# Strassen on column halves in the second layer of the last batch, with two subtractions done by adding transfers

## The chip, the cores and the metric

One NeuronCore of one Trainium2 chip runs the whole program. The metric is the device time of one execution in microseconds; three runs of the kernel before took 2145.92, 2146.27 and 2146.49 us, so the median is 2146.27 us. Engines are named as the profile names them: PE is TensorE (PEld its weight loads), DVE VectorE, ACT ScalarE, POOL GpSimd, and SP the engine that issues the ordinary DMA transfers.

## The reference

Attention over channels and then two dense layers. There are 4 batches of 6080 tokens with 256 channels:

```python
qn = q / (np.linalg.norm(q, axis=1, keepdims=True) + 1e-06)
kn = k / (np.linalg.norm(k, axis=1, keepdims=True) + 1e-06)
s = kn.transpose(0, 2, 1) @ qn / tau
a = np.exp(s - s.max(-1, keepdims=True))
a /= a.sum(-1, keepdims=True) + 1e-09
x = (v @ a).reshape(B * S, D)          # 24320 x 256
h = x @ w_in                           # 256 -> 2048
g = h - np.tanh(h)
return g @ w_out                       # 2048 -> 256
```

## The kernel before

The softmax matrix of a batch is folded into `w_in`, so that the first layer is one product of `v` with folded weights. All data are fp32; each operand of a large product is split into a high part `h` and a low part `l` (an ACT cast and a DVE subtraction), and one product is three matmuls: high weights by low data, high by high, low by high.

Tokens are taken in *pairs* of two column chunks: five *even* pairs of 512 + 512 tokens and one *uneven* pair of 512 + 448 per batch. The hidden layer is taken in 8 slices of 256. One slice of one pair is a *quad*: 2 x 2 blocks (row of 128 hidden units, column chunk of tokens), numbered 11, 12, 21 and 22. There are 4 x 6 x 8 = 192 quads. In the names, `x_3_2_4` is the buffer `x` of batch 3, pair 2, slice 4.

In a quad the first layer is done by Strassen's scheme: seven products p1 to p7 of three matmuls each (21 matmuls of 512 columns, in `products`, L314), accumulated in three PSUM banks X, Y and Z. `Quad.keep` (L1090, ACT) copies X into SBUF before the next product is added to it; `Quad.add` (L1100, DVE) adds such a copy to Y or Z and gives a chunk `c`; chunk 21 is left in X itself. `Quad.finish` turns a chunk into `g = c - tanh(c)`: tanh on ACT (L1112), subtraction on DVE (L1116), high part on ACT (L1120), low part on DVE (L1124). X and Z change between banks 0 and 2 from quad to quad, Y is bank 1.

The second layer (`second`, L1185) multiplies each of the four chunks of `g` by the rows of `w_out` that belong to it: 2 output halves x 3 matmuls of 512 columns, 24 in a quad. The sums over all 8 slices of a pair stay in banks 3 to 6, and are copied out (L1204) and stored (L1207) at its end. Bank 7 is for other work.

`Moving` brings in the tokens of a pair: a load of 1 MB (`vraw`), three subtractions that make `vt` (L882, L885, DVE), and seven splits into `v0` to `v6`.

The order of all instructions is laid down by a planner in the program itself: `ORDER` and `drain` mix the products of the first layer with matmuls of the second, which lags behind by `LAG` matmuls, and `Plan.order` walks through all operations with assumed costs and lists each engine's operations by assumed start. Each engine then runs its own list strictly in order, with semaphores between engines. Where an operation has to wait, all behind it on that engine wait too. In the last batch no attention work for a following batch is left.

Of the kernel before, what the change touches and what calls it, by code (L numbers as in the profile page):

```python
# [43 lines left out]
]  # L44
ENTER = 10
# [47 lines left out]
class Plan:  # L93
# [11 lines left out]
    LONG_LAG, BUSY = 4.5, 180.0  # L105

# [43 lines left out]
    def order(self):  # L150
        ops = self.ops
        for op in reversed(ops):
            if op.due is None:
                op.due = 1e9
            for d in op.deps:
                if d.engine != "PE" or d.fill:
                    d.due = min(1e9 if d.due is None else d.due, op.due - d.cost - self.LAG[d.engine] - self.HOP)
# [28 lines left out]
        while len(done) < len(ops):  # L186
# [66 lines left out]
def attn_moe(ctx: ExitStack, tc: tile.TileContext, qk, v4, qkT, tau, w_in, w_out, outT):  # L253
# [21 lines left out]
    pairs_of = [[*pairs[:MID], pairs[-1], *pairs[MID:-1]] if b + 1 < B else pairs for b in range(B)]  # L275
# [167 lines left out]
    factor = {}  # L443

# [30 lines left out]
    class Attn:  # L475
# [385 lines left out]
    class Moving:  # L861
# [15 lines left out]
        def sums(self, i):  # L877
            n = self.n
            r = self.raw[:, :, 0:n]
            if i == 0:  # L880
                self.t = sb(v_p, "vt", [P, 4, NMAX], F32, f"vt_{self.b}_{self.p}")
                nc.vector.tensor_sub(self.t[:, 0:2, 0:n], r[:, 1:3, :], r[:, 0:2, :])  # L882
            else:
                t = self.t[:, :, 0:n]
                nc.vector.tensor_sub(t[:, i + 1, :], r[:, i + 1, :], t[:, 0 if i == 1 else 2, :])  # L885
# [13 lines left out]
        def split_lo(self, i):  # L899
            nc.vector.tensor_sub(self.lo[i], self.source(i), self.hi[i].bitcast(F32))  # L900
# [133 lines left out]
    def plan_moving(i, after=()):  # L1034
# [3 lines left out]
        plan.add("SP", 0.35, v.load, writes=[raw], after=after, size=1.05)  # L1038
        for j in range(3):
            plan.add("DVE", dve_cost(n if j else 2 * n), lambda j=j: v.sums(j), reads=[raw], writes=[t])  # L1040
        vbuf[i] = {}
        for j in range(7):
            h = Buf(ring["vhl"])
# [3 lines left out]
            plan.add("DVE", dve_cost(v.width(j)), lambda j=j: v.split_lo(j), reads=[src, h], writes=[l])  # L1047
            vbuf[i][j] = h, l


    def banks(gs):

        return {"X": 2 * (gs % 2), "Y": 1, "Z": 2 - 2 * (gs % 2)}

    class Quad:
# [47 lines left out]

        def finish(self, i, c):

            n, name = self.ns[i % 10 - 1], f"{i}_{self.name}"
            t, h, l = Buf(ring["t"]), Buf(ring["gh"]), Buf(ring["gl"])
            self.bufs["g", i] = h, l

            def tanh():  # L1110
                self.tiles["t", i] = sb(g_p, "t", [P, NMAX], F32, f"t{name}")[:, 0:n]
                nc.scalar.activation(self.tiles["t", i], self.tiles[c][:, 0:n], AF.Tanh)  # L1112
# [44 lines left out]

    stream = []
    outs = {}
    obufs = {}  # L1160

    def second(quad, i):

        b, p, s = quad.b, quad.p, quad.s
# [16 lines left out]
        for m, part, x, j in parts:  # L1181
# [47 lines left out]
    for i in range(1, B * NP):  # L1229
        task(NS2 * i - 5, "start", lambda i=i: plan_moving(i, [plan.last_pe]))  # L1230
# [245 lines left out]
    current = None  # L1476
# [110 lines left out]
```

## Time and profile before

| | |
|---|---|
| median of 3 runs | 2146.27 us |
| profiled execution: span, first to last instruction | 2144.3 us |
| PE busy | 2139.4 us, 9666 matmuls |
| DVE busy | 1820.5 us |
| ACT busy | 1578.8 us |
| POOL busy | 37.1 us |
| granted TensorE clock (of 2.4 GHz) | 1.000 |

The page gives the profiled execution by its span alone; the median of the runs is 2.0 us above it. Busy times of DVE and ACT are sums of intervals in which an instruction is in the engine from start to end; the next one can start a little before that end. A busy PE is modelled, so whether PE waited is read from the distance of matmul starts, not from its share. Idle time of the engines beside PE costs nothing as long as PE goes on.

### The profile page before, as it was taken

Reading aid. Unit: us, or ns where it says so; the run is one execution under the profiler, and the core shown is the slowest. Engines: PE = TensorE matmul, PEld = TensorE weight load, DVE = VectorE, ACT = ScalarE, POOL = GpSimd, SP = SyncE. Lnnn points to the kernel's source line nnn. Section 1 sums busy time; section 2 is a strip of 40 time slices with the busy share of each in tenths; the row PEclk is TensorE's granted clock in tenths of the full one; section 3 lists DMA queues with packets and bytes.
Section 4 is the critical chain, followed back from the end, with each engine's and each line's share of the span. In section 5 each row is a group of like instructions: output and inputs, shape, how many; then the busy total and the mean of one; then the engine's idle time right before and its main releaser. Section 6 shows DMA issues by size and latency. Waiting matters only on the chain.

```text
span 2144.3 us, 28289 instructions
## 1 busy us (share of the span) xinstructions
PE 2139.4 (100%) x9666; PEld 1793.2 (84%) x9666; DVE 1820.5 (85%) x3094; ACT 1578.8 (74%) x2922; POOL 37.1 (2%) x37
## 2 busy tenths in 40 slices
PE   9999999999999999999999999999999999999999
PEld 8888888888888888888888888888888888888888
DVE  8998988888898888888889888888888978778776
ACT  6677878767777788886777788887677676666665
POOL 5100000000000000000000000000000000000000
PEclk9999999999999999999999999999999999999999
DMA  9845676355335576643633567564354332332331
GB/s 384 303 163 194 201 265 214 139 160 192 119 134 196 209 246 214 216 156 109 203 131 126 180 237 250 184 227 157 111 196 147 133 126 93 137 125 87 132 117 53
DMA packets 125458, 373.51 MB, mean 174 GB/s; under 512 B 18626, under 2 KB 60866, under 8 KB 122242
## 3 DMA queue, kind: packets, MB, share of 16 engines
q1 hardware_dynamic: 125314, 371.70, 49.3%
q8 instruction: 76, 1.25, 0.2%
q14 instruction: 68, 0.56, 0.1%
HBM read 308.22 MB, written 62.66 MB: 173 GB/s over the span
## 4 chain that ended last, share of the span: by engine, by line
PE 99%; DMA 0%; SPq 0%; ACT 0%; issue 0%
PE ps_o L1185 48%; PE x L314 25%; PE y L314 12%; PE z L314 7%; PE ps_s L314 3%; PE ps_s L602 2%; PE ps_s L600 1%; PE ps_w L314 1%; DMA vhl<-qk_dram 0%; SPq L542 0%; SPq L349 0%; PE ps_n L534 0%; ACT ob L1204 0%; PE ps_b L680 0%; PE ps_t L724 0%
## 5 line engine op out<-in xcount | busy, mean ns | idle before, releaser
L314 PE MATMUL x<-v,f 128*128 128x512 f32 (+1 forms) x2304 | 620.4, 389 | 0.0
L1185 PE MATMUL ps_o<-gh,wo_l 128*128 128x512 f32 (+1 forms) x1536 | 594.9, 387 | 0.0
L1185 PE MATMUL ps_o<-gh,wo_h 128*128 128x512 f32 (+1 forms) x1536 | 594.9, 387 | 0.0
L1124 DVE TENSOR_TENSOR gl<-t,gh 128x512 fp32r<-128x512 f32 (+1 forms) x768 | 508.0, 680 | 22.5 <-ACT gh L1120 20.6
L314 PEld LDWEIGHTS x<-v,f 128*128 128x128 f32 x2304 | 432.6, 188 | 86.3
L1120 ACT CAST gh<-t 128x512 fp32r<-128x512 f32 (+1 forms) x768 | 457.9, 617 | 33.7 <-DVE t L1116 22.7
L1185 PE MATMUL ps_o<-gl,wo_h 128*128 128x512 f32 (+1 forms) x1536 | 470.5, 387 | 0.0
L1112 ACT ACTIVATE t<-c 128x512 f32<-128x512 f32 (+1 forms) x576 | 359.3, 626 | 122.1 <-DVE c L1100 115.4
L1116 DVE TENSOR_TENSOR t<-c,t 128x512 f32<-128x512 f32 (+1 forms) x576 | 389.8, 680 | 37.3 <-ACT t L1112 28.3
L1090 ACT COPY u<-x 128x512 f32<-128x512 f32 (+1 forms) x384 | 221.9, 578 | 209.4 <-PE x L314 207.7
L1100 DVE TENSOR_TENSOR c<-u,y 128x512 f32<-128x512 f32 (+1 forms) x384 | 259.1, 675 | 113.1 <-ACT u L1090 75.2
L1185 PEld LDWEIGHTS ps_o<-gl,wo_h 128*128 128x128 f32 x1536 | 288.4, 188 | 57.2
L1185 PEld LDWEIGHTS ps_o<-gh,wo_l 128*128 128x128 f32 x1536 | 288.4, 188 | 56.3
L1185 PEld LDWEIGHTS ps_o<-gh,wo_h 128*128 128x128 f32 x1536 | 288.5, 188 | 56.2
L314 PE MATMUL y<-v,f 128*128 128x512 f32 (+1 forms) x1152 | 319.0, 385 | 0.0
L314 PEld LDWEIGHTS y<-v,f 128*128 128x128 f32 x1152 | 215.1, 188 | 40.3
L1112 ACT ACTIVATE t<-x 128x512 f32<-128x512 f32 x192 | 114.8, 598 | 133.4 <-PE x L314 132.6
L1116 DVE TENSOR_TENSOR t<-x,t 128x512 f32<-128x512 f32 x192 | 132.6, 691 | 73.1 <-ACT t L1112 72.4
L1100 DVE TENSOR_TENSOR c<-p,z 128x512 f32<-128x512 f32 x192 | 131.7, 686 | 49.1 <-PE z L314 45.6
L314 PE MATMUL z<-v,f 128*128 128x512 f32 x576 | 161.8, 389 | 0.0
L314 PEld LDWEIGHTS z<-v,f 128*128 128x128 f32 x576 | 108.1, 188 | 22.5
L1090 ACT COPY p<-x 128x512 f32<-128x512 f32 x192 | 112.7, 587 | 5.9 <-PE x L314 2.0
(168 smaller groups left out, 1455.2 us busy)
## 6 DMA issues: line engine op xcount, KB each, us to landing
f<-f_d SPq DMA_DIRECT2D x160, 896.0 KB, 4.6
raw<-qk_dram SPq DMA_DIRECT2D x104, 384.0 KB, 5.0
nt<-qkT_dram SPq DMA_DIRECT2D x96, 380.0 KB, 5.1
f_d<-f SPq DMA_DIRECT2D x32, 896.0 KB, 3.9
vraw<-v_dram SPq DMA_DIRECT2D x24, 1024.0 KB, 7.3
outT_dram<-ob SPq DMA_DIRECT2D x88, 256.0 KB, 3.2
wt<-wt_d SPq DMA_DIRECT2D x24, 512.0 KB, 6.8
wt<-wi_d SPq DMA_DIRECT2D x36, 256.0 KB, 5.1
```

The source lines that it names most:

```text
L314: ins = nc.tensor.matmul(out, w, x, start=first and i == 0, stop=last and i == len(seq) - 1, skip_group_check=True,)
L600: nc.tensor.matmul(self.ps[:, 0:C], x[:, 1, k], x[:, 0, q], start=False, stop=last, skip_group_check=True)
L602: nc.tensor.matmul(self.ps.rearrange("p (a c) -> p a c", a=2), x[:, 0, k], x[:, :, q], start=first, stop=False, skip_group_check=True,)
L1090: nc.scalar.copy(self.tiles[to], self.tiles["X"][:, 0:n])
L1100: nc.vector.tensor_add(self.tiles[i], self.tiles[u], self.tiles[ps][:, 0:n])
L1112: nc.scalar.activation(self.tiles["t", i], self.tiles[c][:, 0:n], AF.Tanh)
L1116: nc.vector.tensor_sub(x, self.tiles[c][:, 0:n], x)
L1120: nc.scalar.copy(self.g[i][0], self.tiles["t", i])
L1124: nc.vector.tensor_sub(self.g[i][1], self.tiles["t", i], self.g[i][0].bitcast(F32))
L1185: nc.tensor.matmul(outs[key + (m,)][:, 0:n], (wo_l if part else wo_h)[:, f, m * P:(m + 1) * P], quad.g[i][x], start=first and j == 0, stop ...
```

## The change

It concerns the 40 quads of the even pairs of the last batch (`halved`: batch 3, pair index above 0). For that the uneven pair of this batch is moved from its last place to its first.

The two chunks of the first column, 11 and 21, are taken together as a 2 x 2 block problem: two rows (slices of 128 hidden units) by two halves of 256 columns, against the 2 x 2 blocks of `w_out`. It is done by seven products of three matmuls with 256 columns (21 matmuls of 256 columns) in place of 12 matmuls of 512. The sums of weight blocks are made once in batch 0 (`Sums`), kept in DRAM, and loaded for each of the 40 quads (512 KB, `load_sums`). The sums of data blocks are four DVE subtractions of 256 columns a quad (`Quad.sums`, buffer `ts`). What is split into high and low parts is then `b1` (256 columns), `b2`, `t1` and `t2` (512 each) in place of `gh11/gl11` and `gh21/gl21`. The seven products are summed over the 8 slices in halves of banks 3, 4, 2 and 7, and at the end of a pair put together by two ACT copies and eight DVE additions of 256 columns (`gather_halves`). Banks 2 and 7 being taken, X is always bank 0, and Y and Z share bank 1.

For chunks 11 and 12 of these quads the subtraction `c - tanh(c)` is not done on DVE: ACT writes `-tanh(c)`, and a transfer issued by POOL adds `c` to it in SBUF (`join`, 256 KB).

```diff
+HALVES = [
+    ("p6", []), ("p2", [5, "c"]), ("p5", []), ("p7", [5]), ("p4", ["d", 3]), ("p3", ["a", 4]), ("p1", ["b", 5.5]),
+]
+JOINED = [(),(11,12)]
+SUMS_AT = 3 * 8
...
+    JOIN_LAG, JOIN_SHARE = 4.5, 1.45
...
-    pairs_of = [[*pairs[:MID], pairs[-1], *pairs[MID:-1]] if b + 1 < B else pairs for b in range(B)]
+    pairs_of = [[*pairs[:MID], pairs[-1], *pairs[MID:-1]] if b + 1 < B else [pairs[-1], *pairs[:-1]] for b in range(B)]
...
+        def whole(self):
...
+            nc.vector.tensor_add(self.w, wo_h[:, part].bitcast(F32), wo_l[:, part].bitcast(F32))
+        def sums(self):
...
+            nc.vector.tensor_add(y[:, 0], a21, a22)
+            nc.vector.tensor_sub(y[:, 1], y[:, 0], a11)
+            nc.vector.tensor_sub(y[:, 2], a11, a21)
+            nc.vector.tensor_sub(y[:, 3], a12, y[:, 1])
...
+    def load_sums(gs):
...
+        nc.sync.dma_start(so[gs].bitcast(F32), so_d[s].rearrange("p h (i m) -> p h i m", i=4))
...
-        def sums(self, i):
+        def sums(self, i, eng):
...
-                nc.vector.tensor_sub(self.t[:, 0:2, 0:n], r[:, 1:3, :], r[:, 0:2, :])
+                eng.tensor_sub(self.t[:, 0:2, 0:n], r[:, 1:3, :], r[:, 0:2, :])
...
+        name, cost, eng = ("DVE", dve_cost, nc.vector)
         for j in range(3):
-            plan.add("DVE", dve_cost(n if j else 2 * n), lambda j=j: v.sums(j), reads=[raw], writes=[t])
+            plan.add(name, cost(n if j else 2 * n), lambda j=j: v.sums(j, eng), reads=[raw], writes=[t])
...
+            if j not in POOLED:
+                name, cost, eng = "DVE", dve_cost, nc.vector
+            plan.add(name, cost(v.width(j)), lambda j=j, eng=eng: v.split_lo(j, eng), reads=[src, h], writes=[l])
+            if halved(i // NP, i % NP):
+                name, cost, eng = "POOL", pool_cost, nc.gpsimd
...
+    def halved(b, p):
+        return b == B - 1 and p > 0
...
+        if halved(*where(gs)[:2]):
+            return {"X": 0, "Y": 1, "Z": 1}
...
+                def join():
+                    nc.gpsimd.dma_start(self.tiles["n", i], self.tiles[c][:, 0:n], accum_op=ALU.add)
+                plan.add("ACT", act_cost(n), tanh, reads=[self.bufs[c]], writes=[g])
+                plan.add("POOL", 1.0, join, reads=[self.bufs[c]], writes=[g], port=False, lag=plan.JOIN_LAG)
...
+                    (y[:, 0], g(1, 1), g(1, 0)), (y[:, 1], g(2, 1), g(1, 1)), (y[:, 2], g(2, 1), y[:, 0]), (y[:, 3], g(2, 0), y[:, 2]),
+                )[i]
+                nc.vector.tensor_sub(out, a, b)
...
+    HALF_BANKS = {"p1": (3, 0), "p2": (3, 1), "p3": (4, 0), "p5": (4, 1), "p7": (2, 0), "p6": (2, 1), "p4": (7, 0)}
+    PRODUCTS = {
+        "b1": [("p1", (0, 0), 0)], "b2": [("p2", (1, 0), 0), ("p3", 3, 1)],
+        "t1": [("p5", 0, 0), ("p7", 2, 1)], "t2": [("p6", 1, 0), ("p4", (1, 1), 1)],
+    }
...
+                    nc.tensor.matmul(
+                        outs[b, p, place][:, at_ * HALF:(at_ + 1) * HALF], weights(a, part), quad.g[name][x][:, half * HALF:(half + 1) * HALF],
...
+        if halves_from - 4 <= gs < halves_from:
+            lag += 3
+        if gs == halves_from:
+            lag += 2
```

`lambda j=j: v.sums(j, eng)` reads `eng` when it runs, after the loop below it has set it to `nc.gpsimd` for the halved pairs: the three `vt` subtractions of a halved pair are planned as DVE work and issued on POOL.

How it moves instructions. On PE, from p6 to p7 of one quad (`x` by `v1` is p6, `z` p2, `y` by `v3` p5, `x` by `v4` p7; `ps_o` and `ps_h` are the second layer). Before:

```order
L314 MATMUL x_3_2_4_18959<-v1_3_2_18499,f_164_18814 128x512 x3
L314 MATMUL z_3_2_4_19000<-v2_3_2_18522,f_164_18814 128x512 x3
L1185 MATMUL ps_o_3_2_1_0_18764<-gh12_3_2_2_18915,wo_l_96 128x512
L1185 MATMUL ps_o_3_2_1_0_18764<-gh12_3_2_2_18915,wo_h_95 128x512
L1185 MATMUL ps_o_3_2_1_1_18769<-gh12_3_2_2_18915,wo_l_96 128x512
L1185 MATMUL ps_o_3_2_1_1_18769<-gh12_3_2_2_18915,wo_h_95 128x512
L314 MATMUL y_3_2_4_19016<-v3_3_2_18536,f_164_18814 128x512 x3
L1185 MATMUL ps_o_3_2_1_1_18769<-gl12_3_2_2_18926,wo_h_95 128x512
L1185 MATMUL ps_o_3_2_1_0_18764<-gl12_3_2_2_18926,wo_h_95 128x512
L314 MATMUL x_3_2_4_18959<-v4_3_2_18548,f_164_18814 128x512 x3
```

and now:

```order
L326 MATMUL x_3_2_4_19310<-v1_3_2_18337,f_164_19099 128x512 x3
L326 MATMUL z_3_2_4_19347<-v2_3_2_18195,f_164_19099 128x512 x3
L1376 MATMUL ps_h_3_2_4_19084<-t1_3_2_2_19239,sl_162_19138 128x256 x2
L1376 MATMUL ps_h_3_2_2_19115<-t1_3_2_2_19239,sl_162_19138 128x256 x3
L1376 MATMUL ps_h_3_2_2_19115<-t2_3_2_2_19276,sl_162_19138 128x256 x3
L1376 MATMUL ps_h_3_2_7_19127<-t2_3_2_2_19276,wo_h_95 128x256 x2
L326 MATMUL y_3_2_4_19370<-v3_3_2_18353,f_164_19099 128x512 x3
L326 MATMUL x_3_2_4_19310<-v4_3_2_18360,f_164_19099 128x512 x3
L1376 MATMUL ps_h_3_2_7_19127<-t2_3_2_2_19276,wo_l_96 128x256
```

Between p2 and p5 stand ten matmuls of 256 columns in place of four of 512, and p5 writes the bank that p2 wrote.

On DVE, from c12 of one quad to c11 of the next. Before:

```order
L1100 TENSOR_TENSOR c12_3_2_4_19073<-u2_3_2_4_19006,y_3_2_4_19016 128x512
L1124 TENSOR_TENSOR gl22_3_2_4_19080<-t22_3_2_4_19049,gh22_3_2_4_19069 128x512
L1124 TENSOR_TENSOR gl21_3_2_4_19086<-t21_3_2_4_19060,gh21_3_2_4_19075 128x512
L1116 TENSOR_TENSOR t12_3_2_4_19083<-c12_3_2_4_19073,t12_3_2_4_19083 128x512
L1100 TENSOR_TENSOR c11_3_2_5_19105<-p1_3_2_5_19066,z_3_2_5_19095 128x512
```

and now (`b2`, `glb1` and `gl22` are low parts, `ts` the sums of data halves, `n11` the chunk that the transfer of POOL has added to):

```order
L1166 TENSOR_TENSOR c12_3_3_3_20255<-u2_3_3_3_20186,y_3_3_3_20206 128x512
L1290 TENSOR_TENSOR t22_3_3_3_20249<-c22_3_3_3_20230,t22_3_3_3_20249 128x512
L1219 TENSOR_TENSOR b2_3_3_3_20258<-n21_3_3_3_20251,b2_3_3_3_20258 128x512
L1239 TENSOR_TENSOR ts_3_3_3_20276<-n11_3_3_3_20204 128x256
L1239 TENSOR_TENSOR ts_3_3_3_20276<-n21_3_3_3_20251,n11_3_3_3_20204 128x256
L1219 TENSOR_TENSOR glb1_3_3_3_20291<-n11_3_3_3_20204,ghb1_3_3_3_20280 128x256
L1239 TENSOR_TENSOR ts_3_3_3_20276<-n21_3_3_3_20251,ts_3_3_3_20276 128x256
L1298 TENSOR_TENSOR gl22_3_3_3_20302<-t22_3_3_3_20249,gh22_3_3_3_20285 128x512
L1166 TENSOR_TENSOR c11_3_3_4_20309<-p1_3_3_4_20271,z_3_3_4_20298 128x512
```

Between c12 and the next c11 stand seven operations in place of three, four of them of 256 columns.

`vt` and the transfers. Before, on DVE, where the tokens of pair 3 are prepared:

```order
L882 TENSOR_TENSOR vt_3_3_19004<-vraw_3_3_18906 128x1024
L1100 TENSOR_TENSOR c11_3_2_4_19014<-p1_3_2_4_18969,z_3_2_4_19000 128x512
L1124 TENSOR_TENSOR gl12_3_2_3_19020<-t12_3_2_3_18986,gh12_3_2_3_19009 128x512
L900 TENSOR_TENSOR v0_3_3_18992<-vraw_3_3_18906,v0_3_3_18992 128x512
L1116 TENSOR_TENSOR t11_3_2_4_19022<-c11_3_2_4_19014,t11_3_2_4_19022 128x512
L885 TENSOR_TENSOR vt_3_3_19004<-vraw_3_3_18906,vt_3_3_19004 128x512
```

and now, on POOL, where those of pair 4 are:

```order
L1181 DMA n11_3_3_2_20085<-c11_3_3_2_20068 128x512
L933 TENSOR_TENSOR vt_3_4_20103<-vraw_3_4_19923 128x1024
L1286 DMA t12_3_3_1_20099<-c12_3_3_1_20009 128x512
L936 TENSOR_TENSOR vt_3_4_20103<-vraw_3_4_19923,vt_3_4_20103 128x512
L1286 DMA t12_3_3_2_20149<-c12_3_3_2_20139 128x512
L1181 DMA n11_3_3_3_20204<-c11_3_3_3_20193 128x512
L1286 DMA t12_3_3_3_20266<-c12_3_3_3_20255 128x512
L936 TENSOR_TENSOR vt_3_4_20103<-vraw_3_4_19923,vt_3_4_20103 128x512
L1181 DMA n11_3_3_4_20319<-c11_3_3_4_20309 128x512
```

The three subtractions have gone to POOL, between two transfers a quad that this engine issues in order.

## Rows read from the trace of the kernel before

**Rows 1.** The page: span, busy time, PE clock, chain by engine.

```profile
span 2144.3 us, 28289 instructions
...
PE 2139.4 (100%) x9666; PEld 1793.2 (84%) x9666; DVE 1820.5 (85%) x3094; ACT 1578.8 (74%) x2922; POOL 37.1 (2%) x37
...
PEclk9999999999999999999999999999999999999999
...
PE 99%; DMA 0%; SPq 0%; ACT 0%; issue 0%
```

**Rows 2.** Chain of the last batch in time: start us, us, what, matmuls.

```profile
1991.48 1.36 PE x L314 x6
...
1999.64 2.04 PE ps_o L1185 x9
2001.68 1.36 PE x L314 x6
```

**Rows 3.** Windows: us, busy us of PE, PEld, DVE, ACT, POOL; PE clock, DMA share, GB/s.

```profile
140.00:180.00 40.00, 40.00 (x180) 33.19 (x179) 39.83 (x69) 31.70 (x60) 0.41 (x1) 1.00 0.44 155
...
430.00:600.00 170.00, 170.00 (x752) 140.81 (x751) 145.61 (x259) 119.47 (x211) 0.41 (x1) 1.00 0.46 154
770.00:870.00 100.00, 100.00 (x481) 86.74 (x481) 86.16 (x151) 82.47 (x170) 0.41 (x1) 1.00 0.65 221
...
1710.00:2060.00 350.00, 350.00 (x1545) 289.89 (x1544) 277.59 (x433) 238.01 (x419) 0.00 (x0) 1.00 0.33 119
```

**Rows 4.** Chain at the first folds, columns as in rows 2.

```profile
71.38 4.31 PE ps_w L314 x36
```

**Rows 5.** Groups by shape: line, engine, operation, names, shapes, count, busy us, mean ns.

```profile
L1124 DVE TENSOR_TENSOR gl<-t,gh 128x512 fp32r<-128x512 f32 x704 | 470.8, 686 | 15.2 <-ACT gh L1120 14.1
...
L882 DVE TENSOR_TENSOR vt<-vraw 128x1024 f32<-128x1024 f32 x24 | 29.3, 1220 | 0.0
...
L616 DVE TENSOR_TENSOR s<-s,ps_s 128x256 f32<-128x256 f32 x8 | 3.3, 416 | 0.0
...
L831 DVE TENSOR_TENSOR fx<-fx 128x128 f32<-128x128 f32 x32 | 9.1, 285 | 0.0
```

**Rows 6.** Timeline of one quad of the last batch: start us, us, engine, line, operation.

```profile
1999.68 0.59 ACT L1090 COPY u<-x 128x512 f32<-128x512 f32 x1 [1.30 <-PE x L314]
...
2000.30 0.69 DVE L1100 TENSOR_TENSOR c<-u,y 128x512 f32<-128x512 f32 x1 [1.20 <-ACT u L1090]
...
2001.02 0.63 ACT L1112 ACTIVATE t<-c 128x512 f32<-128x512 f32 x1 [0.23 <-DVE c L1100]
...
2001.52 1.52 PE L314 MATMUL x<-v,f 128*128 128x512 f32 x6
...
2002.46 0.60 ACT L1112 ACTIVATE t<-x 128x512 f32<-128x512 f32 x1 [0.81 <-PE x L314]
...
2003.09 0.69 DVE L1116 TENSOR_TENSOR t<-x,t 128x512 f32<-128x512 f32 x1 [0.71 <-ACT t L1112]
```

**Rows 7.** Timeline of POOL, columns as in rows 6.

```profile
41.22 1.38 POOL L373 TENSOR_TENSOR a_wi<-a_wi,m_wi 128x512 f32<-128x512 f32 x1 [2.73 <-DVE m_wi L370]
...
45.48 1.27 POOL L524 TENSOR_TENSOR acc<-vhl,acc 128x512 f32<-128x512 f32 x1
```

**Rows 8.** Timeline of DVE, columns as in rows 6.

```profile
41.52 1.64 DVE L363 SCALAR_TENSOR_TENSOR a_wi<-raw_wi,a_wi 128x512 int32<-128x512 int32 x1
43.08 3.67 DVE L524 TENSOR_TENSOR acc<-vhl,acc 128x512 f32<-128x512 f32 x6
```

**Rows 9.** DMA issues of 1700 to 2130 us: count, KB each, median us to landing.

```profile
f<-f_d SPq DMA_DIRECT2D x40, 896.0 KB, 4.5
outT_dram<-ob SPq DMA_DIRECT2D x20, 256.0 KB, 2.4
vraw<-v_dram SPq DMA_DIRECT2D x4, 1024.0 KB, 6.8
```

**Rows 10.** The page, DMA issues: columns as in rows 9.

```profile
wt<-wi_d SPq DMA_DIRECT2D x36, 256.0 KB, 5.1
```

**Rows 11.** Timeline at the program's end, columns as in rows 6.

```profile
2139.49 2.06 SPq L1207 DMA_DIRECT2D outT_dram<-ob  x4
...
2140.66 0.53 ACT L1204 COPY ob<-ps_o 128x448 f32<-128x448 f32 x1 [0.62 <-PE ps_o L1185]
```

More of the change, by code (lines that the diff above doesn't have):

```diff
@@ L111, in __init__, with add @@
         self.last_pe = None
-    def add(self, engine, cost, run, reads=(), writes=(), after=(), due=None, size=0, port=None, fill=False, late=0.0):
+    def add(self, engine, cost, run, reads=(), writes=(), after=(), due=None, size=0, port=None, fill=False, late=0.0, lag=0.0):
         op = Op(engine, cost, run, size, engine in ("DVE", "POOL") if port is None else port)
+        op.lag = lag
         op.i = len(self.ops)
@@ L1104, in finish, with sums_late, place @@
+        def sums_late(self, late):
+            self.bufs["t13"], was = late, self.bufs["t13"]
+            late.writers = list(was.writers)
+            self.sums(2)
+            self.sums(3)
+            self.bufs["t13"] = was
+        def place(self, k):
+            return PIECES[((self.gs - halves_from) * 3 + k) % len(PIECES)]
         def finish(self, i, c):
+            if halved(self.b, self.p) and i % 10 == 1:
+                return self.first_column(i)
             n, name = self.ns[i % 10 - 1], f"{i}_{self.name}"
+            apart = self.joined(i)
@@ L1126, in finish @@
             plan.add("ACT", act_cost(n), tanh, reads=[self.bufs[c]], writes=[t])
-            plan.add("DVE", dve_cost(n), sub, reads=[self.bufs[c]], writes=[t], port=not isinstance(c, str))
+            if apart:
+                plan.add("POOL", 1.0, join, reads=[self.bufs[c]], writes=[t], port=False, lag=plan.JOIN_LAG)
+            else:
+                plan.add("DVE", dve_cost(n), sub, reads=[self.bufs[c]], writes=[t], port=not isinstance(c, str))
             plan.add("ACT", act_cost(n), hi, reads=[t], writes=[h])
@@ L1461, in attn_moe, with plan_sums, plan_load_sums @@
             task(12 + 6 * (2 * q + j), "start", lambda q=q, j=j: plan_combine(q, j))
+    sobuf = {}
+    summed = {}
+    def plan_sums(s):
+        c = Sums(s)
+        y, x = Buf(ring["nt"]), Buf(ring["raw"])
+        plan.add("DVE", dve_cost(2 * C), c.whole, writes=[x], after=[plan.last_pe, *wobuf[s].writers])
+        plan.add("DVE", 4 * dve_cost(P), c.sums, reads=[x], writes=[y])
+        plan.add("ACT", act_cost(4 * P), c.hi, reads=[y], writes=[x])
+        plan.add("DVE", dve_cost(4 * P), c.lo, reads=[y], writes=[x])
+        summed[s] = plan.add("SP", 0.35, c.keep, reads=[x], size=0.52, due=plan.pe_time + 40.0)
+    def plan_load_sums(gs):
+        sobuf[gs] = Buf(ring["qh"])
+        plan.add("SP", 0.35, lambda: load_sums(gs), writes=[sobuf[gs]], after=[plan.last_pe, summed[gs % NS2]], size=0.52)
+    for s in range(NS2):
+        task(SUMS_AT + s, "start", lambda s=s: plan_sums(s))
+    for gs in range(halves_from, TOTAL):
+        task(gs, "start", lambda gs=gs: plan_load_sums(gs))
     for b in range(1, B):
```

217 lines of the change are left out of this document (192 added, 25 removed).

## The prediction

> **What bounds the kernel now.** I read the page first: the chain that ended last is PE for 99% of the span, at the full clock in every slice [rows 1]. The chain in time then gives the price of PE's work in the last batch: nine matmuls of 512 columns in 2.04 us, 0.2267 us each, and from one quad to the next 2001.68 - 1991.48 = 10.20 us [rows 2]. A quad has 45 matmuls, and 45 x 0.2267 = 10.20, so PE waits for nothing there. The windows say the same of long stretches, and that the other engines are covered: from 1710 to 2060 us DVE is busy for 277.59 of 350 us, and from 140 to 180 us even 39.83 of 40, while PE goes on [rows 3]. So the change gains what it takes out of PE's queue, and loses what it makes PE wait.
>
> **PE's own work.** 12 matmuls of 512 columns become 21 of 256. The only stretch of 256-column matmuls with fp32r operands that PE runs back to back, each with its own weight load, is that of the first folds: 36 in 4.31 us, 0.1197 us each [rows 4]. That is 21 x 0.1197 = 2.514 us for 12 x 0.2267 = 2.720 us, 0.206 us less in a quad, and **8.25 us less** over 40 quads. The new quad takes 33 x 0.2267 + 2.514 = 9.995 us. The gain is gone at 0.1295 us a matmul, 8% above the row. Nothing else can be won in these quads, since PE does not wait there now.
>
> **Hand-offs of PSUM banks.** X is now always bank 0 and Y and Z share bank 1, so four times a quad PE writes a bank that another engine must first have read. What such a step takes is in one quad of before [rows 6]: six matmuls start at 2001.52, the first three (p4) have their slots until 2002.20, and ACT starts to read X at 2002.46, 0.26 us later; a tanh from PSUM takes 0.60, DVE starts 0.03 after it, a subtraction takes 0.69, a copy 0.59. I set these against the new order, in us from the start of p6: p6 to 0.68, p2 to 1.36, ten halves to 2.56, p5 to 3.24, p7 to 3.92, one half and five full to 5.17, p4 to 5.85, one full and three halves to 6.44, p3 to 7.12, four full to 8.02, the next p1 to 8.70, two full and seven halves to 9.99.
> p2 to p5: DVE adds from 1.62 to 2.31, p5 is due at 2.56, slack 0.25.
> p7 to p4: ACT copies from 4.18 to 4.77, due 5.17, slack 0.40.
> p4 to the next p1: tanh 6.11 to 6.71, subtraction 6.74 to 7.43, due 8.02, slack 0.59.
> p1 to p6: copy 8.96 to 9.55, due 9.99, slack 0.44.
> How long a release takes back to PE no row shows; from ACT to DVE it is 0.03. With the reader free in time all four fit, and I cost them at nothing. From above: 0.2 us in every quad is 8 us, a rival below.
>
> **DVE and ACT.** DVE operations of 512 columns start 0.60 us apart when they follow each other ((3.67 - 0.69) / 5) [rows 8], though each lasts 0.686; one of 256 lasts 0.416 and so takes 0.33 [rows 5]. A halved quad has ten of the first and five of the second, 7.65 us; the splits of the next pair add 7 x 0.60 / 8 = 0.53, the joining at the end of a pair (8 x 0.33 + 0.60) / 8 = 0.41. That is 8.6 of 10.0 us, less than stretches in which PE does not wait [rows 3]. In the order of one quad, DVE is through with the low part of 22 at 11.15 on the clock above, and c11 of the next quad can start at 11.62: 0.47 us idle before the tightest hand-off. ACT gets one and a half casts more a quad, some 0.9 us, on 238 of 350 [rows 3]: hidden. The weight sums in batch 0 are, for each of 8 slices, two operations of 512 and four of 128 columns (0.285, so 0.20 each): 8 x 2.0 = 16 us of DVE, without a date; from 430 to 600 us alone DVE idles for 24 [rows 3, 5]. Cost 0, at most 16 if that cover were gone. The uneven pair in the first place does the same work beside the last folds: 0, at most 2.
>
> **The adding transfers.** They close a loop from one c11 to the next: add 0.69, hop 0.03, tanh 0.63 [rows 6], then L from there until the transfer has landed, then on DVE, in order, two sums, the low part of b1, a third sum and the low part of 22 (4 x 0.33 + 0.60 = 1.92), behind which the next c11 stands. 3.27 + L must fit into 9.995, so **PE waits from L = 6.7 us on**, and then as much longer in every quad as L is above it. The transfer of chunk 12 has about as long until ACT, in order, wants to cast it. No row shows an adding transfer or one issued by POOL. Nearest rows: a store of 256 KB in the last batch lands after 2.4 us, a 1 MB load after 6.8 [rows 9]; loads of 256 KB in busier parts after 5.1 [rows 10]. I take 4.5, near the upper 256 KB row, as the target is read too and POOL has to issue: cost 0; both ends stay for the range. Traffic rises by 0.52 MB of weight sums and 2 x 0.26 MB of transfers a quad, from 119 to 225 GB/s (275 if the read target counts); at 221 GB/s, from 770 to 870 us, PE does not wait [rows 3].
>
> **The subtractions that went to POOL.** While POOL subtracts from 41.22 to 42.60 [rows 7], a DVE operation on two SBUF inputs that would take 0.69 takes 1.64 from 41.52 on [rows 8]: it waits until POOL is done. The Trainium skill (SBUF — State Buffer, "SBUF: two separate sides") calls the port pair of the two engines an exclusive lock, and these rows agree; by that rule POOL's vt work speaks against the change. Five pairs have three such operations, 1.27 us for 512 columns [rows 7] and up to twice that, 2.54, for 1024, which took DVE 1.22 [rows 5]. By the order and the clock above: the wide one stands behind the transfer of chunk 11 and runs from about 4.0 to 6.5; it holds up the low part of t2, n21 starts 0.3 us late, inside its slack. The second runs at about 7.4 and holds t22 for 0.5 us, which the idle 0.47 takes. The third stands behind the transfer of chunk 12, runs from about 9.8 to 11.1, and pushes c11 from 11.62 to 12.4: 0.75 late, less the 0.2 of the hand-off, 0.55 us of PE. The first such pair is prepared during uneven quads, whose banks are not shared. So 4 x 0.55 = **2.2 us more**; from below 0, from above 5 x 5.08 = 25.
>
> **The end.** From the last ACT copy (2140.66 + 0.53) to the end of the span are 3.1 us [rows 11], as after the change; but SP issues the store of that copy first and the other half behind it, at 2.06 / 4 = 0.5 an issue: **0.4 us more**. The last transfer of chunk 12 has 6.2 us before PE wants it.
>
> **The sum.** -8.25 + 2.2 + 0.4 = -5.65 us on a span of 2144.3. The median of the runs is 2.0 above the span, and I leave that as it is: 2146.27 - 5.65 = **2140.6 us**.
>
> **Rivals.** What these runs can tell from no change is about 0.2%, 4.3 us: 2142.0 to 2150.6.
> *The hand-offs eat the gain.* DVE cannot be interrupted; an operation of 0.60 begun just before p2 ends delays c11 by more than the 0.25 of slack. For it: 86% load, and an order laid down with assumed costs. Against it: the idle 0.47 ahead of c11. At 0.1 to 0.2 us a quad it costs 4 to 8 us: 2144.6 to 2148.6, no measurable change. Half matmuls at 0.13 us would end there too.
> *The transfers come late (slower).* Place: the first sum on DVE, waiting for the transfer of chunk 11, with the next c11 behind it. It decides from L = 6.7 us; slower by over 0.2% from 6.7 + (5.65 + 4.3) / 40 = 6.95; at 7.5 it costs 0.8 x 40 = 32 us, 2172. For it: 5.1 and 6.8 us in rows 9 and 10, two transfers a quad beside 1.4 MB of loads, and POOL's in-order queue with vt in it. Against it: 2.4 us for the same size in the same batch.
> *Issuing the transfers locks DVE out* for some 1 us, like a POOL operation, twice a quad. DVE then has 10.6 us of work in 10.0: 0.6 x 40 = 24 us, 2164.6. The same section of the Trainium skill says that GpSimd writes the descriptors of its transfers through that port pair; no run here shows whether a DVE subtraction meets them.
> *No lock cost at all:* 2138.4, the better edge of the forecast.
>
> **Chances.** Forecast 0.52 (its own range 2138.0 to 2142.0); hand-offs 0.27; late transfers 0.14; issue lock 0.07. Faster 0.52, same 0.27, slower 0.21. The range goes from 2137.8 (no lock cost, and none at the end: 2138.0) up through the no-change case to 2153, L = 7.0; above that lie the rest of the last two cases, some 0.16.
>
> **What would show it.** Right: chain pieces of halves at 0.12 us a matmul, p6 to p6 10.0 us, no PE wait in steady quads, DVE operations of over 1.3 us beside POOL's vt, landings of n<-c under 6.7 us. Wrong: quads above 10.1 us. Then the wait of DVE's first sum for a transfer names the late transfers, DVE operations stretched beside POOL's issues the lock, and PE waits before p5, p4, p6 or p1 the hand-offs.

## The result and the profile after

The changed kernel took 2161.89 us (median of 4 runs, 2160.66 to 2162.65), the kernel before 2146.14 on the same chip: a ratio of 1.0074, 95% interval 1.0059 to 1.0088. It is slower by 15.8 us, where the forecast was 2140.6 with a range up to 2153.0. The profiled execution's span grew from 2144.3 to 2160.9 us.

The page answers to [rows 1]. PE is busy longer though it has less to do; POOL has gone from 37.1 to 134.1 us, and the chain that ended last breaks off after some 16% of the span, so it cannot say what bounds the last batch:

```profile
span 2160.9 us, 29501 instructions
...
PE 2142.3 (99%) x10026; PEld 1803.5 (83%) x10026; DVE 1888.3 (87%) x3317; ACT 1616.4 (75%) x3015; POOL 134.1 (6%) x132
...
q1 hardware_dynamic: 132226, 396.87, 52.5%
q0 software_dynamic: 11520, 20.98, 5.4%
...
PE 12%; DVE 2%; DMA 1%; issue 1%; ACT 0%; POOL 0%; SPq 0%; ACTq 0%; POOLq 0%
```

The windows (us, busy us of PE, PEld, DVE, ACT, POOL; clock, DMA share, GB/s) say where to look: in the stretch of [rows 3] PE is no longer busy throughout, in the last pair, for which nothing more is prepared, it is:

```profile
1710.00:2060.00 350.00, 340.40 (x1772) 289.29 (x1771) 312.14 (x553) 257.39 (x477) 75.29 (x74) 1.00 0.73 209
...
2088.00:2128.00 40.00, 40.00 (x215) 34.48 (x215) 33.14 (x63) 29.19 (x54) 7.21 (x9) 1.00 0.75 207
```

A steady quad from the timeline of PE (start us, us, engine, line, operation), from the p2 of one quad (`z`) to the next. It answers to the quad of 10.20 us in [rows 2] and the halves of [rows 4]:

```profile
2099.07 0.85 PE L326 MATMUL z<-v,f 128*128 128x512 f32 x3
2099.76 1.12 PE L1376 MATMUL ps_h<-t,sl 128*128 128x256 f32 x8
2100.72 0.40 PE L1376 MATMUL ps_h<-t,wo_h 128*128 128x256 f32 x2
2100.95 0.86 PE L326 MATMUL y<-v,f 128*128 128x512 f32 x3
2101.65 0.85 PE L326 MATMUL x<-v,f 128*128 128x512 f32 x3
2102.34 0.28 PE L1376 MATMUL ps_h<-t,wo_l 128*128 128x256 f32 x1
2102.45 0.40 PE L1453 MATMUL ps_o<-gh,wo_l 128*128 128x512 f32 x1
...
2103.61 0.84 PE L326 MATMUL x<-v,f 128*128 128x512 f32 x3
...
2109.15 0.63 PE L326 MATMUL z<-v,f 128*128 128x512 f32 x2
```

Ten halves take 2100.95 - 2099.76 = 1.19 us, 0.119 each, as forecast. But the quad takes 10.08 us, not 9.995: the full matmuls that follow halves start further apart, five of them 2103.61 - 2102.45 = 1.16 us in place of 1.133, three of them 0.69 or 0.70 in place of 0.68. So the gain is 0.12 x 40 = 4.8 us instead of 8.25.

Now a quad in which the next pair is prepared: z starts at 1921.33 and next at 1933.61, 12.28 us instead of 10.08. In brackets is the idle time before an instruction and what ended it:

```profile
1921.33 0.85 PE L326 MATMUL z<-v,f 128*128 128x512 f32 x3
...
1924.36 3.39 DVE L1239 TENSOR_TENSOR ts<-n,ts 128x256 f32<-128x256 f32 x1
1924.73 2.72 POOL L933 TENSOR_TENSOR vt<-vraw 128x1024 f32<-128x1024 f32 x1
...
1927.67 0.68 DVE L1166 TENSOR_TENSOR c<-u,y 128x512 f32<-128x512 f32 x1
1927.68 1.93 POOL L936 TENSOR_TENSOR vt<-vraw,vt 128x512 f32<-128x512 f32 x1
...
1928.40 0.53 PEld L326 LDWEIGHTS y<-v,f 128*128 128x128 f32 x3 [1.32 <-DVE c L1166]
...
1928.43 1.75 DVE L1219 TENSOR_TENSOR t<-ts,t 128x512 fp32r<-128x512 f32 x1
1930.10 0.68 DVE L1194 TENSOR_TENSOR n<-x,t 128x512 f32<-128x512 f32 x1
...
1930.83 0.53 PEld L326 LDWEIGHTS x<-v,f 128*128 128x128 f32 x3 [0.98 <-DVE n L1194]
...
1933.61 0.63 PE L326 MATMUL z<-v,f 128*128 128x512 f32 x2
```

A sum of 256 columns that normally takes 0.42 us takes 3.39: it ends 0.3 us after POOL's wide subtraction. Behind it in DVE's order stands chunk 22 (`c<-u,y`), which frees Y, and PE waits 1.32 us for it. POOL's second subtraction stretches a low part from 0.69 to 1.75, chunk 21 (`n`) comes late, X is not free, and PE waits 0.98. The third comes at the end of the next quad. It holds a sum ahead of c11 of the quad behind that, and p5 of that quad waits 0.95 us:

```profile
1942.45 2.10 DVE L1239 TENSOR_TENSOR ts<-n,n 128x256 f32<-128x256 f32 x1
...
1942.64 1.62 POOL L936 TENSOR_TENSOR vt<-vraw,vt 128x512 f32<-128x512 f32 x1
...
1946.48 0.53 PEld L326 LDWEIGHTS y<-v,f 128*128 128x128 f32 x3 [0.95 <-DVE c L1166]
```

The Trainium skill (SBUF — State Buffer, "SBUF: two separate sides") says that of a GpSimd operation and a DVE operation with two SBUF inputs, the one that starts first has the shared pair for its whole length; these rows agree on the length, 3.39 us against 0.42. On who is first they do not quite: by the records the sum starts 0.37 us ahead of POOL's operation and still waits, but the spans of POOL are rough.

That is how the time is lost in two of the four later pairs. In the other two a part of it goes another way, through POOL's list: the transfer of chunk 12 stands behind the wide subtraction (in one pair behind the second too), is issued some 2 us later than in the first experiment below (counted from the transfer of chunk 11 ahead of it), and lands after 5.9 and 7.0 us instead of 3.4 and 4.2. ACT waits 2.66 and 2.98 us for it, and in its order the copy that frees X stands behind that cast, so PE waits 1.20 and 1.60 us for X. The chain of one of them (start us, us, what):

```profile
1842.34 2.41 POOL vt L933
1844.76 7.04 DMA t<-c
...
1851.82 0.02 ACT gh L1294
...
1852.35 0.59 ACT u L1156
...
1852.98 0.96 PE x L326 x3
```

What the quads of the four later pairs take beyond 10.08 us, by the starts of their `z`, is 4.71 + 2.57 + 3.22 + 3.13 = 13.6 us, of which 1.3 remain when `vt` is not on POOL (first experiment). Some 3 us of the rest are the two late transfers of chunk 12. The first such pair, prepared in an uneven quad with X and Z still changing banks, costs more than any other: that quad took 14.63 us, against 9.97 without POOL's `vt`. PE waited 3.10 us in one piece; in the five microseconds after, the mean granted clock was 0.70, so PE ran a part of them at 1.2 GHz:

```profile
1685.00:1690.00 5.00, 2.28 (x10) 1.64 (x9) 5.00 (x7) 1.13 (x2) 0.58 (x1) 0.95 0.31 129
1690.00:1695.00 5.00, 5.00 (x17) 4.03 (x17) 3.71 (x8) 2.56 (x6) 0.00 (x0) 0.70 0.13 54
```

By their medians the adding transfers came in time (count, KB each, median us to landing, 1750 to 2150 us; beside [rows 9, 10]):

```profile
sl<-so_d SPq DMA_DIRECT2D x38, 512.0 KB, 3.3
t<-c POOLq DMA_DIRECT2D x39, 256.0 KB, 4.2
n<-c POOLq DMA_DIRECT2D x38, 256.0 KB, 3.8
```

Not all did: of the 80, seven took 7.0 to 8.7 us, over the 6.7 that the prediction allows. One is that of the chain above; the other six were issued where a pair ends and the next pair's 1 MB is loaded. For two of these DVE's first sum waited, 0.57 us at 1752.69 and 0.97 at 1837.76, and PE then waited 1.09 and 0.77 us before p5.

At the end, in place of [rows 11], the last copy ends at 2156.26 + 0.59, 4.05 us before the end of the span (3.1 before): 0.95 more.

```profile
2155.72 1.01 SPq L1408 DMA_DIRECT2D outT_dram<-ob  x2
...
2156.26 0.59 ACT L1476 COPY ob<-ps_o 128x512 f32<-128x512 f32 x1 [2.88 <-PE ps_o L1453]
2156.87 0.86 SPq L1479 DMA_DIRECT2D outT_dram<-ob  x2
```

The account of the 16.6 us between the two spans: the subtractions on POOL 13.6 - 1.3 + 14.63 - 9.97 = 17.0 (some 3 of it by late transfers behind them, 0.8 by the late transfer of chunk 11 at 1837.76, which was issued before that pair's subtractions, the other 13, by difference, by the lock, with the clock that it cost); two waits in the first halved pair that stay without them, 1.8; a start of the last batch that is 1.4 late (1635.70 against 1634.32 for the same `z`); the end 0.95; halves -4.8. That makes 16.4.

### The profile page after: what moved, and what is told of

It is laid out like the page before. It is cut to its first block, busy times and chain, and to the rows that moved or that the text cites. A ratio compares the mean times of both kernels' runs of the same rounds, so it can differ in the third digit from the quotient of the medians.

```text
span 2160.9 us, 29501 instructions
## 1 busy us (share of the span) xinstructions
PE 2142.3 (99%) x10026; PEld 1803.5 (83%) x10026; DVE 1888.3 (87%) x3317; ACT 1616.4 (75%) x3015; POOL 134.1 (6%) x132
## 3 DMA queue, kind: packets, MB, share of 16 engines
q1 hardware_dynamic: 132226, 396.87, 52.5%
q0 software_dynamic: 11520, 20.98, 5.4%
## 5 line engine op out<-in xcount | busy, mean ns | idle before, releaser
L1453 PE MATMUL ps_o<-gh,wo_l 128*128 128x512 f32 (+1 forms) x1376 | 533.4, 388 | 0.3 <-ACT gh L1294 0.3
L1453 PE MATMUL ps_o<-gh,wo_h 128*128 128x512 f32 (+1 forms) x1376 | 533.4, 388 | 0.0
L1298 DVE TENSOR_TENSOR gl<-t,gh 128x512 fp32r<-128x512 f32 (+1 forms) x688 | 460.3, 686 | 24.2 <-ACT gh L1294 23.3
L1294 ACT CAST gh<-t 128x512 fp32r<-128x512 f32 (+1 forms) x688 | 412.3, 616 | 39.4 <-DVE t L1290 20.9
L1453 PE MATMUL ps_o<-gl,wo_h 128*128 128x512 f32 (+1 forms) x1376 | 427.9, 387 | 0.0
L1283 ACT ACTIVATE t<-c 128x512 f32<-128x512 f32 x536 | 333.7, 624 | 99.3 <-DVE c L1166 90.2
L1290 DVE TENSOR_TENSOR t<-c,t 128x512 f32<-128x512 f32 (+1 forms) x496 | 335.0, 680 | 24.7 <-ACT t L1283 19.5
L1453 PEld LDWEIGHTS ps_o<-gh,wo_l 128*128 128x128 f32 x1376 | 258.4, 188 | 52.2 <-DVE ob L1476 0.9
L1453 PEld LDWEIGHTS ps_o<-gl,wo_h 128*128 128x128 f32 x1376 | 258.1, 188 | 52.0 <-DVE gl L1298 0.8
L1453 PEld LDWEIGHTS ps_o<-gh,wo_h 128*128 128x128 f32 x1376 | 258.4, 188 | 49.0
```

Of the source, the lines that this page charges most:

```text
L1290: nc.vector.tensor_sub(x, self.tiles[c][:, 0:n], x)
L1294: nc.scalar.copy(self.g[i][0], self.tiles["t", i])
L1298: nc.vector.tensor_sub(self.g[i][1], self.tiles["t", i], self.g[i][0].bitcast(F32))
L1453: nc.tensor.matmul(outs[key + (m,)][:, 0:n], (wo_l if part else wo_h)[:, f, m * P:(m + 1) * P], quad.g[i][x], start=first and j == 0, stop ...
```

## The experiments

Each ratio is to the kernel before on the same chip, with its 95% interval.

**The three subtractions back on DVE.** One binding, the rest of the program in the same order:

```diff
-            plan.add(name, cost(n if j else 2 * n), lambda j=j: v.sums(j, eng), reads=[raw], writes=[t])
+            plan.add(name, cost(n if j else 2 * n), lambda j=j, eng=eng: v.sums(j, eng), reads=[raw], writes=[t])
```

> The changed kernel with its three vt subtractions on DVE, where the planner had put them; nothing else moves. Theory (POOL's vt locks DVE, and the shared banks pass that on to PE): the PE waits beside vt go, some 17.2 us, and the lost clock after the longest of them, some 1.4, so a span of 2160.9 - 18.6 = 2142.3 and runs of about 2143.5 (2142 to 2145), that is 0.997 to 0.9995 of the kernel before; quads beside vt at 10.1 to 10.3 us. Rival A (the transfers or DVE's load at the preparation of a pair are to blame, vt only happens to lie there): the waits stay, 2155 or more. Rival B (vt on DVE costs what it cost on POOL, since 2.4 us of DVE work a pair have no room): 2148 to 2155.

Measured: 2144.66 us, ratio 0.9994 (0.9985 to 1.0003), span 2142.9. That is 17.2 us less than the changed kernel, and the clock is full again. In the last batch PE waits of 0.5 us or more are left in two places, none beside `vt`: 0.55 and 1.26 us, both in the first halved pair. The theory stands, both rivals fall. What the run does not separate is the lock from POOL's list: with `vt` on DVE no transfer stands behind a subtraction either. What is left of the change, 1.4 us, is less than a measurement of this kernel can tell from nothing.

**The same move in the kernel before.** 

```diff
         def sums(self, i):
             n = self.n
+            eng = nc.gpsimd if self.b == B - 1 and self.p < NP - 1 else nc.vector
...
-                nc.vector.tensor_sub(self.t[:, 0:2, 0:n], r[:, 1:3, :], r[:, 0:2, :])
+                eng.tensor_sub(self.t[:, 0:2, 0:n], r[:, 1:3, :], r[:, 0:2, :])
...
-                nc.vector.tensor_sub(t[:, i + 1, :], r[:, i + 1, :], t[:, 0 if i == 1 else 2, :])
+                eng.tensor_sub(t[:, i + 1, :], r[:, i + 1, :], t[:, 0 if i == 1 else 2, :])
```

> The kernel before, with the vt subtractions of the last batch's even pairs on POOL and still planned as DVE work. Theory (a lock costs PE only where the next bank waits for DVE at once): DVE operations beside vt stretch to 2 to 3 us here too, but X changes banks from quad to quad and DVE has idle time to make it up, so PE loses 0 to 4 us: ratio 1.000 to 1.002. Rival (the lock alone is enough): three waits of 1 us in each of 5 pairs, 12 to 17 us, ratio 1.006 to 1.008.

Measured: 2147.33 us, ratio 1.0006 (0.9997 to 1.0015), 1.3 us more. The lock is there (an operation of 0.69 us takes 2.71), but in the even quads PE waits for nothing; its only waits, 0.85 and 0.89 us, stand where a pair is prepared beside the last folds. To see whether it is DVE's load that makes the difference, the next kernel had the low part of chunk 22 formed twice as well, which raises DVE to 85% in the even quads (85.06 of 100 us from 1780 to 1880, with the time in which it is held; in the changed kernel 88.44):

```diff
-                nc.vector.tensor_sub(self.g[i][1], self.tiles["t", i], self.g[i][0].bitcast(F32))
+                for _ in range(2 if i == 22 and self.b == B - 1 else 1):
+                    nc.vector.tensor_sub(self.g[i][1], self.tiles["t", i], self.g[i][0].bitcast(F32))
```

> The kernel before with vt of the last batch's even pairs on POOL, as in an earlier run, and one DVE operation of 512 columns more in each of the batch's 48 quads (the low part of chunk 22 is formed twice), so that DVE is as busy as in the changed kernel, some 85%, while X still changes banks from quad to quad. Theory (shared banks pass the lock on to PE): still no PE wait of 1 us beside vt after the folds are over, ratio 1.000 to 1.002, 2146 to 2150. Rival (DVE's load does it, since it leaves no idle time to make up a lock): waits of 1 us and more beside vt, 2152 to 2165.

Measured: 2148.59 us, ratio 1.0012 (1.0003 to 1.0021). DVE is held for 2.71 us and then again, and the even quads stay at 10.20 us; the 2.5 us that are lost stand beside the last folds again, where PE waits 1.84 and 0.88 us:

```profile
1850.34 2.71 POOL L883 TENSOR_TENSOR vt<-vraw 128x1024 f32<-128x1024 f32 x1 [75.39 <-DMA vraw<-v_dram]
1850.88 2.71 DVE L1117 TENSOR_TENSOR t<-c,t 128x512 f32<-128x512 f32 x1
1853.12 3.43 POOL L886 TENSOR_TENSOR vt<-vraw,vt 128x512 f32<-128x512 f32 x2
```

So the lock alone does not lose the time in even quads, nor does it with DVE at 85%: it takes something of the halved quads. That can be the shared banks, the held operation's place ahead of chunk 22, the transfers behind the subtractions in POOL's list, or the few per cent by which DVE is busier still; these runs do not separate them.

**`vt` planned on POOL.** 

```diff
-        name, cost, eng = ("DVE", dve_cost, nc.vector)
+        name, cost, eng = ("POOL", pool_cost, nc.gpsimd) if halved(i // NP, i % NP) else ("DVE", dve_cost, nc.vector)
```

> The changed kernel with vt on POOL and planned there, at POOL's assumed cost and with the planner's rule that POOL and DVE do not work on SBUF at once; so DVE's list no longer counts vt as its own, and other operations are laid beside it. Theory (a lock of up to 2.8 us in one piece is longer than any slack of a hand-off, .25 to .59 us, wherever it is planned): most of the 17 us stays, 2152 to 2164. Rival (the loss is that of an order which does not know of the lock): 2144 to 2147, like the run with vt on DVE.

Measured: 2161.41 us, ratio 1.0072 (1.0058 to 1.0085). An order that knows of the lock saves nothing. Most of PE's waits are for DVE again, in two pairs for the copy of an output bank that stands behind a held low part (2.17 and 2.09 us). The loss is not that of a plan and an issue that disagree.

**`vt` on POOL in eight pieces of 256 columns.** 

```diff
+                if halved(self.b, self.p):
+                    for k, h in ((0, 0), (0, 1), (1, 0), (1, 1)):
+                        x = slice(h * HALF, (h + 1) * HALF)
+                        eng.tensor_sub(self.t[:, k, x], r[:, k + 1, x], r[:, k, x])
+                    return
```

(and the other two in two pieces each)

> The changed kernel, vt on POOL, but in eight operations of 256 columns a pair in place of one of 1024 and two of 512. POOL holds the port as long in sum, or a little longer, but in pieces of some 0.7 to 0.9 us, between which DVE can get one operation in. Theory A (it is the length of one hold against slacks of .25 to .59 that makes PE wait): most of the loss goes, 2146 to 2152. Theory B (it is DVE's lost time in sum, some 6 us a pair): the loss stays, 2158 to 2166.

Measured: 2159.63 us, ratio 1.0063 (1.0048 to 1.0079). By the numbers that is theory B, but the trace shows that the run does not decide: DVE did not get in between the pieces.

```profile
1919.87 3.82 DVE L1245 TENSOR_TENSOR ts<-n,ts 128x256 f32<-128x256 f32 x1
1920.24 3.11 POOL L936 TENSOR_TENSOR vt<-vraw 128x256 f32<-128x256 f32 x4
```

Four operations back to back on POOL held one DVE operation until all four were over. Whether single short holds would cost less stays open.

**No adding transfers** (with `vt` on DVE, as all that follow; `JOINED = [(),()]`).

> vt on DVE, and no adding transfers: DVE does the subtractions of chunks 11 and 12 itself, two more of 0.60 us in each of 40 quads. Theory (transfers are on time and free, and DVE at 8.6 of 10.08 us has room that 9.8 us plus vt no longer leaves): DVE becomes the bound in the quads that prepare a pair and the hand-offs get late in the others; 4 to 25 us slower than the run with vt on DVE and transfers, 2147 to 2168. Rival (the transfers are part of the loss): as fast as that run or faster, 2140 to 2143.

Measured: 2163.6 us, ratio 1.0083 (1.0067 to 1.0098). In the range of the theory, but not for its reason: the quads keep their 10.08 us while DVE does all the subtractions, and the whole loss sits at the ends of pairs, where PE waits for DVE's copy of an output bank, up to 6.16 us. After the two longest of these waits the granted clock is 0.50 for some 4 us, 1.2 GHz, so that the quads took 18.51 and 17.22 us. Two runs with one transfer a quad, `JOINED = [(),(11,)]` and `[(),(12,)]`:

> vt on DVE, and only chunk 11 by an adding transfer: one transfer a quad instead of two, DVE .60 us more a quad. Without transfers PE waited at the end of each pair alone, some 5 us, behind DVE's copies of the output banks (what DVE had not done in eight quads), and steady quads took 10.08. Theory (DVE is behind by its load times the time, and .60 x 8 = 4.8 us a pair less work makes that up): 2144 to 2148, waits at pair ends under 1.5 us. Rival (both transfers are needed; half the relief, half the loss): 2151 to 2157.

> vt on DVE, and only chunk 12 by an adding transfer. Same load of DVE and of the transfers as with chunk 11 alone. Theory: the same time as that run within 1.5 us, with no transfer in the loop from c11 to the next c11; DVE's first sum then waits for nothing. Rival (where the relief lies counts): over 3 us apart.

Measured: chunk 11 alone 2144.03 us, ratio 0.9990 (0.9981 to 1.0000); chunk 12 alone 2169.09, ratio 1.0110 (1.0095 to 1.0125). The theory of equal load falls by 25 us. With chunk 12 alone every pair ends in a stretched quad of some 15 us, and there the chain of waits (start us, us, what) is:

```profile
1996.79 6.14 DMA t<-c
...
2002.95 0.63 ACT gh L1294
...
2003.60 0.69 DVE gl L1298
2004.29 0.61 DVE ob L1476
...
2004.95 1.44 PE ps_o L1453 x4
```

In DVE's list the copy of the output bank has got behind a low part that waits for the transfer. With chunk 11 joined the copy stands ahead of them and PE waits 0.17 us. So a transfer of chunk 11 is worth some 20 us because of where the planner then puts one copy, and the one of chunk 12 nothing.

**A third adding transfer a quad**, chunk 22 (`JOINED = [(),(11,12,22)]`); the second of the two runs has also the order of halves of the next paragraph.

> vt on DVE, and chunk 22 by an adding transfer as well, halves in the order of the changed kernel. Theory: DVE had no waits to give back but the two in the first halved pair (1.8 us in sum), of which one follows a late transfer, so nothing or up to 1 us less than the run with vt on DVE: 2143.5 to 2145. Rival (late transfers): 2147 or more.

> vt on DVE, the half matmuls as eleven after p2, and the subtraction of chunk 22 too done by an adding transfer, three a quad in place of two. In the run with eleven after p2 PE waited 1 us or more in two quads that prepare a pair, behind DVE's n21; DVE has .60 us less to do in each quad here. Theory (DVE's time is what is scarce at the preparation of a pair, and transfers cost nothing as long as they land in time): those waits go, quads of 10.06 all through, 2142.5 to 2144. Rival (a third transfer of 256 KB a quad, and 0.25 MB more traffic in 10 us, makes the others late): waits behind casts on ACT, 2147 or more.

Measured: 2190.00 us, ratio 1.0205 (1.0191 to 1.0219), and 2190.57, ratio 1.0201 (1.0187 to 1.0215). This is the rival of the late transfers, 44 us of it. In the first of the two kernels, the landings (1770 to 2110 us):

```profile
t<-c POOLq DMA_DIRECT2D x60, 256.0 KB, 7.0
...
n<-c POOLq DMA_DIRECT2D x30, 256.0 KB, 6.0
```

The group of ACT's casts (count, busy us, mean ns, idle us before them and for what), 1780 to 2110 us:

```profile
L1294 ACT CAST gh<-t 128x512 fp32r<-128x512 f32 x57 | 35.3, 620 | 59.9 <-DMA t<-c 59.6
```

And one window, columns as before:

```profile
1780.00:1880.00 100.00, 91.32 (x476) 75.11 (x475) 75.60 (x143) 66.94 (x125) 23.30 (x27) 1.00 0.90 220
```

With two transfers (`vt` on DVE) the same casts waited 0.6 us, and the same window had a DMA share of 0.77 at 217 GB/s. The transfers of chunks 12 and 22 are issued within 2 us of each other, the DMA engines are at 0.90 with no more GB/s than before, and ACT, in order, holds the copy that frees X behind a cast that waits.

**One switch from half to full matmuls less.**

```diff
-    ("p6", []), ("p2", [5, "c"]), ("p5", []), ("p7", [5]), ("p4", ["d", 3]), ("p3", ["a", 4]), ("p1", ["b", 5.5]),
+    ("p6", []), ("p2", [5.5, "c"]), ("p5", []), ("p7", [5]), ("p4", ["d", 2.5]), ("p3", ["a", 4]), ("p1", ["b", 5.5]),
```

> vt on DVE, and the half matmul that stands alone ahead of five full ones, after p7, moved to the ten after p2: one switch from halves to full matmuls less in a quad, nothing else changed on PE. Theory (a full matmul that follows a half one loses some .021 us, four times a quad, and that is the difference of 10.08 and 9.995): steady quads of 10.06 us, 0.85 less over 40 quads than the run with vt on DVE, 2143.8. Rival (the .085 us is spread over the halves, whatever their order): quads stay at 10.08, 2144.7; other rival (p2 to p5 is the tight hand-off and gets .12 us more): the two waits of .5 and 1.3 us in the first halved pair shrink, up to 1 us more.

Measured: 2145.89 us, ratio 0.9998 (0.9990 to 1.0007). The steady quads take 10.06 us, as the theory of the switches says, but PE waits in two preparing quads (1.13 us at 2009.47, 0.53 at 1763.52), which eats it. Both follow a late transfer of chunk 12. In the chain of the first it lands after 7.52 us, at 2007.45; ACT's cast has waited 1.57 us for it, and behind the low part of that cast DVE has chunk 21. With chunk 11 alone as a transfer:

> vt on DVE, only chunk 11 by an adding transfer, and the half matmuls as eleven after p2 (one switch from half to full matmuls less in a quad). Beside the run with chunk 11 alone, 2144.03, the theory of the switches expects steady quads of 10.06 in place of 10.08, 0.85 less over 40 quads, if the waits that the same move brought with two transfers (some 2 us in two preparing quads) do not come: 2143.2. Rival (the move makes chunk 21 late whatever the transfers): waits of 1 us at the preparation of pairs stay, 2144 to 2146. The kernel before: 2146.1; ratio 0.9986 by the theory.

Measured: 2143.52 us, ratio 0.9987 (0.9978 to 0.9996): quads of 10.06, waits of 0.7 us at most, and no wait of ACT or DVE for a transfer. It is the fastest version, 2.7 us below the kernel before.

**The uneven pair first, in the kernel before.** 

```diff
-    pairs_of = [[*pairs[:MID], pairs[-1], *pairs[MID:-1]] if b + 1 < B else pairs for b in range(B)]
+    pairs_of = [[*pairs[:MID], pairs[-1], *pairs[MID:-1]] if b + 1 < B else [pairs[-1], *pairs[:-1]] for b in range(B)]
```

> The kernel before with one line changed: in the last batch the uneven pair comes first instead of last. Theory: about nothing, between -1 and +2 us (ratio 0.9995 to 1.001). Rival (part of the loss comes from this move, since quad 143 already starts 1.4 us late in the changed kernel, and the uneven quads beside the last folds show a wait): +3 us or more.

Measured: 2146.54 us, ratio 1.0002 (0.9993 to 1.0011). Nothing lost.

## Why the prediction was wrong

*The subtractions on POOL: the step that failed.* "So 4 x 0.55 = 2.2 us more" was 17.0 us. The mechanism was named, and POOL held DVE nearly when assumed; what followed from the holds was wrong.

First, the wide one started 4.1 us after the start of p6, 1924.73 - (1921.33 - 0.69), where 4.0 was assumed, but in two pairs it then held the sum ahead of chunk 22, not the low part behind it. Chunk 22 frees Y for p3. This hand-off was there before the change and so was not among the four that were looked at; by the text's own clock it has 6.44 - 4.77 - 0.69 = 0.98 us of slack, and the hold took that and 1.32 us of PE. In the other two pairs it came some 1 us later, held the low part, as assumed, and cost PE nothing by that.

Secondly, each hold was set against the idle time of a DVE that is on time. The second subtraction ran right behind the wide one (from 7.0, where 7.4 was assumed), DVE was still late, and PE waited 0.98 us for chunk 21. The third ran from 9.7, where 9.8 was assumed, but a quad later, and cost the wait before p5 that the text has, 0.95 us in place of 0.55.

Thirdly, "The first such pair is prepared during uneven quads, whose banks are not shared", which kept that pair out of the sum, is no reason: it cost 4.7 us, the most of all. DVE has the folds beside it (busy for 5.00 of 5 us from 1685), and behind PE's wait of 3.10 us the granted clock of 0.70 took another (1 - 0.70) x 5 = 1.5, an estimate.

Fourthly, the sum looked at DVE alone. POOL's list, with `vt` in it, is named only under the late transfers; there the subtractions made two transfers late, some 3 us.

The upper bound that the text itself gave, 25 us, was nearer than the term.

*PE's own work*, -8.25: mis-sized, -4.8. The half matmul costs 0.119 us as read; that a full one behind it costs more, some 0.02 us a switch and four switches a quad, stood in no row of before, and the row used ran halves alone.

*Hand-offs*, 0: right in steady quads, where nothing waits; in the first halved pair two waits before p5, 1.8 us in sum, of which the longer follows a late transfer.

*DVE's and ACT's load, weight sums, uneven pair first*, 0: right within 0.5 us by the start of the last batch in the first experiment (1.4 in the profiled execution of the changed kernel). That the uneven pair is free was tried by itself.

*Transfers*, 0: right for most, with medians of 3.8 and 4.2 us against the 4.5 taken; not at the ends of pairs, where some took over 7 us and DVE's first sum waited, as the rival says, at a cost of some 2 us. The edge was real and near: with medians of 6.0 and 7.0 us the kernel loses 44 us, though by casts on ACT, not by DVE's first sum.

*The end*, 0.4: 0.95.

*Rivals.* The issue lock is not there. Of the 195 DVE operations that ran beside one of 74 issues of POOL in the first experiment (1740 to 2120 us), none of 512 columns took over 0.70 us and none of 256 over 0.43, such as this one:

```profile
1821.63 0.86 POOL L1181 DMA_DIRECT2D n<-c  x1 [3.35 <-ACT n L1178]
...
1822.11 0.42 DVE L1239 TENSOR_TENSOR ts<-n,ts 128x256 f32<-128x256 f32 x1
```

The rival of no change describes what is left without the subtractions on POOL, though its time goes to switches and two waits and not to hand-offs in every quad.

## What to carry to other kernels

A lock between two engines is not priced by the slack of one steady quad: take the full hold off every hand-off that stands behind the held engine's list, add up holds that follow each other, and look at the stage with the least room, not at the one for which a reason to be safe is at hand. Work that moves to another engine also stands ahead of what that engine has to do: here of transfers. An engine named in a plan and the engine that issues must be the same variable. And where an engine works in order, look at what a moved wait gets in front of: one transfer more or less changed the place of one copy, and that was 20 us.

## What the runs showed of the hardware

A matmul of 512 columns that follows ones of 256 starts the next later than in a run of its like: 10.08 us a quad with four such switches, 10.06 with three.

DVE does not get in between operations that POOL runs back to back: four of 256 columns, 3.11 us together, held one DVE operation of 0.42 us for 3.82 us. What was held had both inputs in SBUF; chunk 22's addition, with one input in PSUM, kept its 0.68 us at 1927.67 beside POOL's second subtraction.

An adding transfer from SBUF to SBUF takes more of the DMA engines than its bytes say: by the page, 20.98 MB of them took 5.4% of the engines' span and 396.87 MB of ordinary ones 52.5%, about twice the share per MB. It fits that a third of them a quad raised the DMA share from 0.77 to 0.90 without more GB/s.
